# Reordering the start of a fused state-space and two-layer kernel, and loading a broadcast matrix in two transfers

## The chip, the cores and the metric

The kernel runs on one core of a Trainium2 chip. A core has five engines with a queue of instructions each: TensorE (PE in the profile; its weight loads stand apart as PEld), VectorE (DVE), ScalarE (ACT), GpSimd (POOL) and SyncE (SP), which here only issues DMAs. Sixteen DMA engines move data between HBM and SBUF. The metric is the device time of one execution in microseconds; the kernel before takes 588.4 us (median of 3 runs, 588.01 to 589.73).

## The reference

Three parts follow each other; all arithmetic is in float32, and no part may be left out.

```python
# 1. attn: x [4, 8, 768, 32], a [4, 8, 768], B and C [4, 8, 768, 16], in chunks of 32 positions
cum = cumsum(log(clip(a, 1e-6, 1)))                        # within a chunk
L = exp(cum_i - cum_j) * (i >= j)
y = ((C B^T) * L) x  +  (C state) * exp(cum)
state = exp(cum_last) * state + sum_j B_j x_j * exp(cum_last - cum_j)
x = y.transpose(0, 2, 1, 3).reshape(3072, 256)
# 2. first layer: w_in [256, 2048], w_out [2048, 256]
h = x @ w_in;  g = where(h > 0, h, exp(min(h, 0)) - 1);  x = g @ w_out
# 3. second layer: w1, w2 [256, 1024], w3 [1024, 1024], w_out [1024, 256]
out = ((x @ w1) * (x @ w2)) @ w3 @ w_out
```

## The kernel before

The 3072 rows are worked on in six tiles of 512 (`TT`), and a tile is made of four chunks of 128 positions (24 chunks in all, two halves of 64 in each). TensorE gets its float32 operands as two words, a high part that it can take at its full rate and the rest: `split` (lines 102 to 104) rounds on ScalarE and subtracts on VectorE or GpSimd, and `mm3` (lines 239 to 242) makes three matmuls of one product.

A chunk goes through four phases (lines 416 to 442): `p0` scans the decays into L (`at_prep`) and scales B with L's last column (`bd`), `p1` multiplies C B^T with L (`at_cb`), `p2` scales C with the decays (`at_cd`, on GpSimd) and advances the two states (`at_u`), `p3` makes y from L and from the states and splits it into xT (`at_y`). Phase p of chunk k has the number 4k + p in `ORDER` (line 37), the list by which the four chunks of the first tile and the first weights are woven; "pr" is the scan of the first tile's decays, "aw" the matmuls that spread a over chunks 2 and 3, and "h" the first half of the first products.

L of the first four chunks comes from such matmuls. From chunk 4 on `at_l` (lines 306 to 312) loads it: each of a chunk's two halves has one row of 512 values in DRAM (`a_cut`), which all 64 partitions of the half get. It is one DMA, whose source has the loops 2 x 64 (a broadcast) x 512. L has three buffers, the chunks' data (`xbc`, 512 KB) four. `p0` of chunk k issues the loads of L for chunk k + 2 and of the data for chunk k + 3.

Weights arrive as 64-bit words in pieces of 512 KB (class `Piece`, lines 121 to 158), and each goes through three stages: `load` (the DMA), `bits` (a shift on VectorE, a scaling on ScalarE, a merge on VectorE) and `parts` (`split`). `queue` holds the pieces in the order in which the steps need them: w_in 0, 1, 2, w_out 0, w_in 3, w_out 1 and so on. An entry (i, stage) of `ORDER` brings piece i up to that stage (2 is `bits`, 3 is `parts`); reaching 3 also issues the load of piece i + 8, which takes the room of an earlier one. The other stages come from `weights_for` (lines 609 to 616), by due times in a planner's clock.

After the attention of the first tile the steps run: unit a (12 matmuls of 512 columns, then exponential, ramp and maximum on ScalarE and VectorE, and a split to g), unit b (12 matmuls into an accumulator), and later c, d and w. The first tile's eight a and b units run with the chunks of the second tile and the weights' stages placed between.

Each engine's instructions run in the order in which a scheduler wrote them, from a simulation of this program. `pace` (lines 115 to 119) tells it to keep an instruction behind the latest mark; marks are the last entries of `last_mm` after each entry of `ORDER` and after each step. `at_prep`, `at_cb` and `at_y` put their VectorE result there for the first four chunks; `at_u` leaves what was there.

Of the kernel before, what the change touches and what calls it, by code (L numbers as in the profile page):

```python
# [10 lines left out]
ALU = mybir.AluOpType  # L11
AX = mybir.AxisListType

NB, NH, S, D, N = 4, 8, 768, 32, 16
Q = 128
SUB = 2
R = Q // SUB
CPB = S // Q
NCHUNK = NB * CPB
TT = 512  # L20
NTILE = NB * S // TT
CPT = TT // Q
# [11 lines left out]
PACE, LATE, END, FIRST = 1.5, 12.0, 7.0, 8.0  # L34
SPILL, BACK = 3, 8

ORDER = [0, 4, 1, "pr", 2, "aw", (0, 2), 5, 3, 6, (0, 3), 8, 7, 9, (1, 2), 10, 12, 11, 13, (1, 3), 14, "h", 15, (2, 2), (3, 2)]


XCOLS = (("x", DM), ("bn", NH * N), ("bt", 2 * R), ("cz", 2 * 2 * R), ("cp", SUB * 2 * R))  # L40
# [3 lines left out]
def kernel(  # L44
# [20 lines left out]
    nc = tc.nc  # L65
# [9 lines left out]
    V, A, G, T = nc.vector, nc.scalar, nc.gpsimd, nc.tensor  # L75
# [23 lines left out]
    def pair(shape, name, tag=None):  # L99
        return [wts.tile(shape, F32R, name=f"{name}_{p}", tag=f"{tag or name}_{p}") for p in ("hi", "lo")]  # L100

    def split(hi, lo, raw, lo_eng):
        A.copy(hi, raw)  # L103
        return lo_eng.tensor_tensor(out=lo, in0=raw, in1=hi.bitcast(F32), op=ALU.subtract)  # L104

    def tmp(name):
        return act.tile([P, 2, TT], F32, tag="tmp", name=name, bufs=TMP)

    def banks(name):

        return ps_w.tile([P, 2, TT], F32, tag="w", name=name)
# [48 lines left out]
    w_in_s = pair([P, 2, F1], "w_in")  # L160
# [7 lines left out]
    early = [0]  # L168
# [68 lines left out]
    last_mm = []  # L237

    def mm3(out, whi, wlo, xhi, xlo, first, last, **kw):
        last_mm[:] = [T.matmul(out, wlo, xhi, start=first, stop=False, **kw).ins]  # L240
        T.matmul(out, whi, xlo, start=False, stop=False, **kw)  # L241
        T.matmul(out, whi, xhi, start=False, stop=last, **kw)  # L242
# [12 lines left out]
    xT = {}  # L255
    state = {}
    a_cut = tc.dram_tile([NCHUNK * SUB, NH, R], F32, name="a_cut")
# [17 lines left out]
    def at_load(k):  # L275
        c = ck[k]
        all_ = att.tile([P, XC], F32, tag="xbc", name=f"xbc{k}", bufs=4)
        nc.sync.dma_start(all_, xc[k])
        cols_ = {}
        at = 0  # L280
        for nm, n in XCOLS:
            cols_[nm] = all_[:, at:at + n]
            at += n
        c["x"], c["bn"] = cols_["x"], cols_["bn"].rearrange("p (h n) -> p h n", h=NH)
        c["bt"] = cols_["bt"].rearrange("p (g j) -> p g j", g=2)
        c["cz"] = cols_["cz"].rearrange("p (g f) -> p g f", g=2)
        c["cp"] = cols_["cp"].rearrange("p (s f) -> p s f", s=SUB)

    pr = {}

    def at_pr(t):

        pr[t] = att.tile([P, CPT * SUB, R], F32, tag="pr", name=f"pr{t}", bufs=2)
        nc.sync.dma_start(pr[t].rearrange("p k i -> p (k i)"),
                          a_h[t].rearrange("h (o s) -> h o s", o=1).to_broadcast([NH, N, TT]))

    def at_decay(t):

        v = pr[t]
        pace(clip(V, v, v))  # L300
        V.tensor_copy(begun[:, :, 0:1], v[:, :, 0:1])
        V.memset(v[:, :, 0:1], 0.0)
        V.tensor_tensor_scan(out=v.rearrange("p k i -> p (k i)"), data0=v.rearrange("p k i -> p (k i)"),
                             data1=begun.rearrange("p k i -> p (k i)"), initial=0.0, op0=ALU.mult, op1=ALU.add)

    def at_l(k):
        c = ck[k]
        c["L"] = att.tile([P, NH, R], F32, tag="L", name=f"L{k}", bufs=3)
        if k >= CPT:
            nc.sync.dma_start(c["L"].rearrange("p h s -> p (h s)"),  # L310
                              a_cut[SUB * k:SUB * k + SUB].rearrange("s h (o i) -> s o (h i)", o=1)
                              .to_broadcast([SUB, R, NH * R]))

    def at_wide(k):


        wide = ps_a.tile([P, 2, TT], F32, tag="acc", name=f"aw{k}") if k else banks(f"aw{k}")
        for j in range(2):
            for p in range(2):
                mm = T.matmul(wide[:, j], sel[:, k + j].rearrange("r s i -> r (s i)"),  # L320
                              cut[0][:, p].rearrange("r h i -> r (h i)"), start=p == 0, stop=p == 1)
                if j == p == 0:
                    tc.keep_in_program_order(mm)
            ck[k + j]["a"] = wide[:, j]
# [44 lines left out]
    def at_u(k):  # L369


        c = ck[k]
        last = k % CPB == CPB - 1
        u = banks(f"u{k}")
        for p in range(4):
            for s in range(SUB - last):
                rows = slice(R * s, R * s + R)
                T.matmul(u[32 * p:32 * p + 32, s, :2 * D], c["bd"][rows, 2 * p:2 * p + 2].rearrange("p h n -> p (h n)"),
                         c["x"][rows, 64 * p:64 * p + 64], start=True, stop=True)
        for s in range(SUB - last):  # L380
            new = att.tile([P, 2 * D], F32, tag="st", name=f"st{k}_{s}", bufs=4)
            if k % CPB or s:
                V.scalar_tensor_tensor(out=new, in0=state[k, s], scalar=c["pr"][:, s, R - 1:R], in1=u[:, s, :2 * D],
                                       op0=ALU.mult, op1=ALU.add)
            else:
                V.tensor_copy(new, u[:, s, :2 * D])
            state[(k, 1) if s == 0 else (k + 1, 0)] = new

    def at_y(k):
        c = ck[k]  # L390
        both = banks(f"y{k}")[:, :, :2 * R].rearrange("p s (g i) -> p s g i", g=2)


        for g in range(2):
            for s in range(SUB):
                rows = slice(R * s, R * s + R)
                for q in range(4):
                    h = 2 * q + g
                    mm = T.matmul(both[32 * q:32 * q + 32, s, g], c["x"][rows, D * h:D * h + D], c["L"][rows, h],
                                  start=g == 0, stop=(k, s) not in state, skip_group_check=True)  # L400
        for g in range(2):
            for s in range(SUB):
                for q in range(4) if (k, s) in state else ():
                    rows = slice(32 * q, 32 * q + 32)
                    mm = T.matmul(both[rows, s, g], state[k, s][rows, D * g:D * g + D], c["cd"][rows, s, g],  # L405
                                  start=False, stop=True, skip_group_check=True)
        last_mm[:] = [mm.ins]
        t, s0 = k // CPT, (k % CPT) * Q
        if k % CPT == 0:
            xT[t] = [act.tile([P, 2, TT], F32R, tag=f"xx{p}", name=f"xT{p}{t}", bufs=3) for p in ("h", "l")]  # L410
        made = split(*(v[:, :, s0:s0 + Q].rearrange("p g (s i) -> p s g i", s=SUB) for v in xT[t]), both, V)
        if k < CPT:
            last_mm[:] = [made.ins]
# [29 lines left out]

    gt, pt, x2, accs = {}, {}, {}, {}

    early_h = []

    def products(h, t, n, cs):
        for j in range(2):
            fs = slice((2 * n + j) * P, (2 * n + j + 1) * P)  # L450
            for k in range(2):
                mm3(h[:, j, cs], w_in_s[0][:, k, fs], w_in_s[1][:, k, fs], xT[t][0][:, k, cs], xT[t][1][:, k, cs],
                    k == 0, k == 1)

    def first_half():

        early_h.append(banks("h0_0"))
        products(early_h[0], 0, 0, slice(0, TT // 2))

    def unit_a(t, n):  # L460

        early = early_h and (t, n) == (0, 0)
        h = early_h[0] if early else banks(f"h{t}_{n}")
        products(h, t, n, slice(TT // 2 if early else 0, TT))
        e = tmp(f"e{t}_{n}")
        A.activation(e, h, AF.Exp)  # L466

        A.activation(e, e, AF.Relu, scale=-1.0, bias=1.0)  # L468
        V.scalar_tensor_tensor(out=e, in0=e, scalar=-1.0, in1=h, op0=ALU.mult, op1=ALU.max)  # L469
        g = act.tile([P, 2, 2, TT], F32R, tag="g", name=f"g{t}_{n}")  # L470
        split(g[:, 0], g[:, 1], e, V)
        gt[t, n] = g
# [64 lines left out]
    made = 0  # L537
# [107 lines left out]
    constants()  # L645
    at_load(0)
    at_pr(0)
    queue[0].advance(1)
    for k in range(1, CPT):
        at_load(k)  # L650
    for p in queue[1:3]:
        p.advance(1)
# [3 lines left out]
    for k in range(CPT):  # L656
        at_l(k)
# [3 lines left out]

    for j in ORDER:
        if j == "pr":
            at_decay(0)
        elif j == "aw":
            at_wide(2)
        elif j == "h":
            first_half()
        elif isinstance(j, tuple):
            i, stage = j  # L670
            queue[i].advance(stage)
            if stage == 3:
                load_next(i)
        else:
            attn[j]()
            marks.extend(last_mm)
    at_pr(1)
    for k in range(CPT, CPT + LOADS):
        if k < CPT + LOADS - 1:
            at_l(k)  # L680
        at_load(k)
# [67 lines left out]
```

## Time and profile before

| | |
|---|---|
| median of 3 runs | 588.4 us |
| the profiled execution | 588.74 us |
| its span, first to last instruction | 587.0 us |
| TensorE busy | 560.5 us, 95% of the span |
| VectorE busy | 336.2 us, 57% |
| ScalarE busy | 277.7 us, 47% |
| GpSimd busy | 83.8 us, 14% |
| loads of L | 20 of 256 KB |
| mean granted TensorE clock | 0.991 of 2.4 GHz |

A row of the timeline gives start and duration in us, the engine, the line of the kernel, the operation, the tile written and those read (their numbers left out), the shapes and how many instructions were merged into the row; in brackets stands the idle time of the engine ahead of it and what ended that. TensorE's matmuls are pipelined, so their distance from start to start is what counts. `L` alone is the decay matrix; `L333` is line 333.

### The profile page before, as it was taken

How to read it: one execution, taken by the hardware profiler on the slowest of the kernel's cores; microseconds unless marked ns; L12 is line 12 of the kernel's file. 1: busy time of each engine (PE TensorE's matmuls, PEld its weight loads, DVE VectorE, ACT ScalarE, POOL GpSimd, SP SyncE). 2: the span in 40 equal slices, each digit the busy share in tenths (PEclk: the TensorE clock that was granted, in tenths of full speed). 3: DMA queues.
4: the chain of work that ended last, by engine and by line, in shares of the span. 5: the costliest groups of instructions: out<-in, count | busy, mean ns of one | idle time of the engine just before them, and what ended most of it. 6: DMA issues, size and time to landing. Idle time of an engine off the chain costs nothing.

```text
span 587.0 us, 10429 instructions
## 1 busy us (share of the span) xinstructions
PE 560.5 (95%) x4436; PEld 439.8 (75%) x4436; DVE 336.2 (57%) x468; ACT 277.7 (47%) x390; POOL 83.8 (14%) x91
## 2 busy tenths in 40 slices
PE   5986799999999999999999999999999999999996
PEld 3665577767877888887788787887777778888784
DVE  6697879677675865668433335343676353335332
ACT  2294567565564655775323223232454552355222
POOL 2201114322222312253000000000021000000000
PEclk9999699999999999999999999999999999999999
DMA  8885353724453331621013031100110000010000
GB/s 297 298 242 155 124 173 111 260 101 126 137 195 96 113 127 73 214 86 58 1 50 113 1 126 37 54 37 1 58 53 1 1 1 0 1 37 2 0 1 36
DMA packets 26567, 52.78 MB, mean 90 GB/s; under 512 B 1592, under 2 KB 9784, under 8 KB 26520
## 3 DMA queue, kind: packets, MB, share of 16 engines
q1 hardware_dynamic: 26520, 52.11, 27.1%
q8 instruction: 35, 0.57, 0.4%
q14 instruction: 12, 0.10, 0.1%
HBM read 45.71 MB, written 6.39 MB: 89 GB/s over the span
## 4 chain that ended last, share of the span: by engine, by line
PE 77%; DMA 10%; DVE 6%; ACT 2%; issue 2%; POOL 1%; SPq 0%; POOLq 0%; DVEq 0%; ACTq 0%
PE ab L240 8%; PE ab L241 7%; PE ab L242 7%; DMA L<-a_cut 6%; PE acc_b L240 6%; PE acc_b L241 6%; PE h L240 6%; PE acc_b L242 6%; PE h L242 5%; PE h L241 5%; PE acc_d L240 4%; PE acc_d L241 4%; PE acc_d L242 4%; PE y L405 2%; DMA raw_wc<-in_w3t 2%
## 5 line engine op out<-in xcount | busy, mean ns | idle before, releaser
L469 DVE SCALAR_TENSOR_TENSOR e<-e,h 128x1024 f32<-128x1024 f32 x48 | 58.4, 1216 | 39.8 <-ACT e L468 39.8
L241 PE MATMUL acc_b<-g,w_out_hi 128*128 128x512 f32 x192 | 77.3, 403 | 3.8 <-DVE g L104 3.8
L240 PE MATMUL acc_b<-g,w_out_lo 128*128 128x512 f32 x192 | 77.9, 406 | 3.1 <-DVE w_out_lo L104 2.1
L240 PE MATMUL h<-xTh,w_in_lo 128*128 128x512 f32 (+1 forms) x196 | 78.1, 399 | 1.9 <-DVE e L469 1.0
L104 DVE TENSOR_TENSOR g<-e,g 128x1024 fp32r<-128x1024 f32 x48 | 61.6, 1283 | 29.0 <-ACT g L103 28.7
L242 PE MATMUL h<-xTh,w_in_hi 128*128 128x512 f32 (+1 forms) x196 | 76.2, 389 | 0.0
L241 PE MATMUL h<-xTl,w_in_hi 128*128 128x512 f32 (+1 forms) x196 | 76.2, 389 | 0.0
L242 PE MATMUL acc_b<-g,w_out_hi 128*128 128x512 f32 x192 | 76.1, 396 | 0.0
L240 PE MATMUL ab<-x2h,w 128*128 128x512 f32 x192 | 74.6, 394 | 0.7 <-ACT x2h L103 0.7
L241 PE MATMUL ab<-x2l,w 128*128 128x512 f32 x192 | 75.0, 391 | 0.0
L103 ACT CAST g<-e 128x1024 fp32r<-128x1024 f32 x48 | 50.4, 1050 | 52.0 <-DVE e L469 38.1
L242 PE MATMUL ab<-x2h,w 128*128 128x512 f32 x192 | 74.8, 389 | 0.0
L466 ACT ACTIVATE e<-h 128x1024 f32<-128x1024 f32 x48 | 49.2, 1026 | 44.2 <-PE h L242 43.0
L514 DVE TENSOR_TENSOR pa<-pa,ab 128x512 f32<-128x512 f32 x48 | 32.6, 684 | 61.2 <-ACT pa L513 61.2
L513 ACT COPY pa<-ab 128x512 f32<-128x512 f32 x48 | 27.9, 589 | 74.4 <-PE ab L242 73.5
L104 DVE TENSOR_TENSOR p<-pa,p 128x512 fp32r<-128x512 f32 x48 | 32.9, 692 | 34.2 <-ACT p L103 33.8
L468 ACT ACTIVATE e<-e 128x1024 f32<-128x1024 f32 x48 | 51.0, 1063 | 0.9
L103 ACT CAST p<-pa 128x512 fp32r<-128x512 f32 x48 | 29.8, 622 | 44.9 <-PE acc_d L242 23.3
L366 POOL TENSOR_TENSOR cd<-xbc,pr 128x256 f32<-128x256 f32 x24 | 24.7, 1028 | 173.9 <-issue 85.8
L240 PEld LDWEIGHTS acc_b<-g,w_out_lo 128*128 128x128 f32 x192 | 36.6, 190 | 13.1 <-DVE w_out_lo L104 2.5
L241 PEld LDWEIGHTS acc_b<-g,w_out_hi 128*128 128x128 f32 x192 | 36.6, 191 | 12.8 <-DVE g L104 5.2
L240 PEld LDWEIGHTS h<-xTh,w_in_lo 128*128 128x128 f32 x196 | 37.2, 190 | 11.5 <-DVE e L469 1.5
(93 smaller groups left out, 898.5 us busy)
## 6 DMA issues: line engine op xcount, KB each, us to landing
xbc<-in_xc SPq DMA_DIRECT2D x24, 512.0 KB, 9.8
raw_wc<-in_w3t SPq DMA_DIRECT2D x16, 512.0 KB, 7.0
L<-a_cut SPq DMA_DIRECT2D x20, 256.0 KB
raw_wi<-in_w_in SPq DMA_DIRECT2D x8, 512.0 KB, 11.9
raw_wo<-in_w_out SPq DMA_DIRECT2D x8, 512.0 KB
out_t<-o SPq DMA_DIRECT2D x12, 256.0 KB, 2.0
raw_wq<-in_wo SPq DMA_DIRECT2D x4, 512.0 KB, 11.5
raw_wb<-in_w SPq DMA_DIRECT2D x4, 512.0 KB
```

The lines of the kernel that those rows point to most:

```text
L103: A.copy(hi, raw)
L104: return lo_eng.tensor_tensor(out=lo, in0=raw, in1=hi.bitcast(F32), op=ALU.subtract)
L240: last_mm[:] = [T.matmul(out, wlo, xhi, start=first, stop=False, **kw).ins]
L241: T.matmul(out, whi, xlo, start=False, stop=False, **kw)
L242: T.matmul(out, whi, xhi, start=False, stop=last, **kw)
L366: G.tensor_tensor(out=c["cd"], in0=c["cp"].rearrange("p s (w i) -> p s w i", w=2), in1=c["pr"].rearrange("p s (o i) -> p s o i", o=1).to_b ...
L405: mm = T.matmul(both[rows, s, g], state[k, s][rows, D * g:D * g + D], c["cd"][rows, s, g], start=False, stop=True, skip_group_check=True)
L466: A.activation(e, h, AF.Exp)
L468: A.activation(e, e, AF.Relu, scale=-1.0, bias=1.0)
L469: V.scalar_tensor_tensor(out=e, in0=e, scalar=-1.0, in1=h, op0=ALU.mult, op1=ALU.max)
L513: A.copy(e, h[:, 0])
L514: V.tensor_tensor(out=e, in0=e, in1=h[:, 1], op=ALU.mult)
```

## The change

There are five edits:

- the early half of the first products goes ("h" in `ORDER`, `first_half`, and the split of `unit_a` in two halves of columns);
- `at_u` sets the mark for the first four chunks, so that paced stages of weights which follow in `ORDER` are kept behind the chunk's last state;
- piece 2 (w_in 2) goes through `bits` and `parts` and piece 3 (w_out 0) through both as well around the last y of the tile; before, only their `bits` stood there, behind that y;
- the data of chunk 1 is loaded ahead of the first piece of weights;
- L of a chunk is loaded by two DMAs of 64 partitions, one for each half.

```diff
-ORDER = [0, 4, 1, "pr", 2, "aw", (0, 2), 5, 3, 6, (0, 3), 8, 7, 9, (1, 2), 10, 12, 11, 13, (1, 3), 14, "h", 15, (2, 2), (3, 2)]
+ORDER = [0, 4, 1, "pr", 2, "aw", (0, 2), 5, 3, 6, (0, 3), 8, 7, 9, (1, 2), 10, 12, 11, 13, (1, 3), 14, (2, 2), (2, 3), 15, (3, 2), (3, 3)]
...
         if k >= CPT:
-            nc.sync.dma_start(c["L"].rearrange("p h s -> p (h s)"),
-                              a_cut[SUB * k:SUB * k + SUB].rearrange("s h (o i) -> s o (h i)", o=1)
-                              .to_broadcast([SUB, R, NH * R]))
+
+            for s in range(SUB):
+                nc.sync.dma_start(c["L"][R * s:R * s + R].rearrange("p h s -> p (h s)"),
+                                  a_cut[SUB * k + s:SUB * k + s + 1].rearrange("s h i -> s (h i)").to_broadcast([R, NH * R]))
...
             if k % CPB or s:
-                V.scalar_tensor_tensor(out=new, in0=state[k, s], scalar=c["pr"][:, s, R - 1:R], in1=u[:, s, :2 * D],
-                                       op0=ALU.mult, op1=ALU.add)
+                made = V.scalar_tensor_tensor(out=new, in0=state[k, s], scalar=c["pr"][:, s, R - 1:R], in1=u[:, s, :2 * D],
+                                              op0=ALU.mult, op1=ALU.add)
             else:
-                V.tensor_copy(new, u[:, s, :2 * D])
+                made = V.tensor_copy(new, u[:, s, :2 * D])
             state[(k, 1) if s == 0 else (k + 1, 0)] = new
+        if k < CPT:
+            last_mm[:] = [made.ins]
...
-    def first_half():
-
-        early_h.append(banks("h0_0"))
-        products(early_h[0], 0, 0, slice(0, TT // 2))
...
-        early = early_h and (t, n) == (0, 0)
-        h = early_h[0] if early else banks(f"h{t}_{n}")
-        products(h, t, n, slice(TT // 2 if early else 0, TT))
+        h = banks(f"h{t}_{n}")
+        products(h, t, n)
...
     at_pr(0)
+    at_load(1)
     queue[0].advance(1)
-    for k in range(1, CPT):
+    for k in range(2, CPT):
         at_load(k)
```

## Rows read from the trace of the kernel before

**Rows 1.** The page: busy tenths of TensorE and VectorE in 40 slices of 14.7 us.

```profile
PE   5986799999999999999999999999999999999996
DVE  6697879677675865668433335343676353335332
```

**Rows 2.** Stages: length, busy us of PE, PEld, DVE, ACT, POOL; clock, DMA share, GB/s.

```profile
30.00:50.00 20.00, 16.52 (x134) 11.91 (x132) 19.84 (x29) 17.59 (x24) 2.05 (x2) 1.00 0.75 217
50.00:60.00 10.00, 6.09 (x58) 4.66 (x50) 6.12 (x11) 2.43 (x4) 2.06 (x3) 0.92 0.62 189
60.00:70.00 10.00, 7.89 (x78) 5.65 (x79) 8.36 (x12) 5.45 (x8) 1.03 (x2) 0.57 0.21 78
150.00:200.00 50.00, 50.00 (x489) 39.74 (x488) 35.63 (x50) 29.85 (x39) 11.28 (x12) 1.00 0.44 139
```

**Rows 3.** The chain of waits, start and length in us, from 19 to 57 us.

```profile
19.86 21.72 DMA L<-a_cut
...
41.64 15.33 DMA L<-a_cut
```

**Rows 4.** The timeline of SyncE, 18 to 31 us.

```profile
18.13 6.73 SPq L310 DMA_DIRECT2D L<-a_cut  x2
24.96 5.05 SPq L278 DMA_DIRECT2D xbc<-in_xc  x1
30.11 0.48 SPq L136 DMA_DIRECT2D raw_wo<-in_w_out  x1
```

**Rows 5.** Stages as in rows 2: chunks and weights loading, then only L.

```profile
18.00:20.00 2.00, 1.47 (x59) 0.86 (x56) 1.99 (x4) 0.56 (x1) 0.45 (x1) 1.00 1.04 382
54.60:56.70 2.10, 1.47 (x29) 0.88 (x27) 0.00 (x0) 0.00 (x0) 0.00 (x0) 1.00 0.13 52
```

**Rows 6.** The timeline of VectorE, 9.5 to 13 us.

```profile
9.50 0.42 DVE L261 TENSOR_SCALAR pr<-pr 128x512 f32<-128x512 f32 x1
9.83 0.42 DVE L146 TENSOR_SCALAR raw_wi<-raw_wi 128x512 uint32<-128x512 uint32 x1
...
10.47 0.68 DVE L148 SCALAR_TENSOR_TENSOR raw_wi<-raw_wi 128x512 uint32<-128x512 uint32 x1
...
11.21 1.22 DVE L303 TENSOR_TENSOR_SCAN pr<-pr,begun 128x512 f32<-128x512 f32 x1
12.35 0.67 DVE L104 TENSOR_TENSOR w_in_lo<-raw_wi,w_in_hi 128x512 fp32r<-128x512 f32 x1
```

**Rows 7.** The timeline of VectorE, 23 to 82 us.

```profile
23.53 0.59 DVE L383 SCALAR_TENSOR_TENSOR st<-st,pr,u 128x64 f32<-128x64 f32 x2
28.09 0.42 DVE L104 TENSOR_TENSOR xTl<-y,xTh 128x256 fp32r<-128x256 f32 x1 [3.97 <-ACT xTh L103]
...
57.00 1.22 DVE L333 TENSOR_TENSOR_SCAN L<-L,eye 128x512 f32<-128x512 f32 x1 [3.88 <-DMA L<-a_cut]
...
62.49 0.68 DVE L104 TENSOR_TENSOR w_out_lo<-raw_wo,w_out_hi 128x512 fp32r<-128x512 f32 x1
...
66.87 1.23 DVE L333 TENSOR_TENSOR_SCAN L<-L,eye 128x512 f32<-128x512 f32 x1 [1.64 <-DMA L<-a_cut]
...
81.88 0.42 DVE L104 TENSOR_TENSOR xTl<-y,xTh 128x256 fp32r<-128x256 f32 x1 [2.08 <-ACT xTh L103]
```

**Rows 8.** The timeline of TensorE, 25 to 65 us.

```profile
25.93 0.68 PE L399 MATMUL y<-L,xbc 64*32 64x64 f32 x32
...
59.98 1.13 PE L351 MATMUL cb<-xbc 32*64 32x128 f32 x16 [3.91 <-issue]
63.22 0.79 PE L240 MATMUL acc_b<-g,w_out_lo 128*128 128x512 f32 x1 [2.11 <-DVE w_out_lo L104]
...
64.24 0.63 PE L242 MATMUL acc_b<-g,w_out_hi 128*128 128x512 f32 x1
64.67 0.63 PE L240 MATMUL acc_b<-g,w_out_lo 128*128 128x512 f32 x1
```

**Rows 9.** The timeline of ScalarE at 30 us.

```profile
30.21 1.04 ACT L466 ACTIVATE e<-h 128x1024 f32<-128x1024 f32 x1
```

More of the change, by code (lines that the diff above doesn't have):

```diff
@@ L444, with products @@
     gt, pt, x2, accs = {}, {}, {}, {}
-    early_h = []
-    def products(h, t, n, cs):
+    def products(h, t, n):
         for j in range(2):
@@ L451, in products @@
             for k in range(2):
-                mm3(h[:, j, cs], w_in_s[0][:, k, fs], w_in_s[1][:, k, fs], xT[t][0][:, k, cs], xT[t][1][:, k, cs],
-                    k == 0, k == 1)
-    def first_half():
-        early_h.append(banks("h0_0"))
-        products(early_h[0], 0, 0, slice(0, TT // 2))
+                mm3(h[:, j], w_in_s[0][:, k, fs], w_in_s[1][:, k, fs], xT[t][0][:, k], xT[t][1][:, k], k == 0, k == 1)
     def unit_a(t, n):
-        early = early_h and (t, n) == (0, 0)
-        h = early_h[0] if early else banks(f"h{t}_{n}")
-        products(h, t, n, slice(TT // 2 if early else 0, TT))
+        h = banks(f"h{t}_{n}")
+        products(h, t, n)
         e = tmp(f"e{t}_{n}")
@@ L666 @@
             at_wide(2)
-        elif j == "h":
-            first_half()
         elif isinstance(j, tuple):
```

## The prediction

> **What bounds the kernel now.** I read the page first. Of TensorE's forty digits only the first five slices (73 us) hold anything but nines: 5, 9, 8, 6, 7 [rows 1]. So only the head can give something. A table by stages confirms it: from 150 us on TensorE fills its stretch (50.00 of 50.00), while in 50 to 60 it works 6.09 of 10 us and in 60 to 70 the granted clock is 0.57 [rows 2]. What TensorE does after 70 us moves as one block; the question is how much sooner the head delivers it.
>
> In the head I followed the chain of waits. It holds two pieces of pure transfer: L from a_cut, 21.72 us from 19.86, and the next L, 15.33 us from 41.64 [rows 3]. Each moves 256 KB. SyncE's timeline shows the same from the other side: the two L issues at 18.13 hold it for 6.73 us, and the chunk data behind them hold it another 5.05 us [rows 4]. Then I asked for a stretch in which only L is under way: from 54.6 to 56.7 us the DMA share is 0.13, that is 2 of 16 engines, at 52 GB/s, against 1.04 and 382 GB/s while whole chunks and weights are loaded [rows 5]. So a load of L as written runs on two engines, and whatever is queued behind it is complete only when those two get to it.
>
> VectorE's timeline says what that costs. VectorE stands still for 3.97 us before 28.09, for 3.88 us before the scan of L at 57.00 and for 1.64 us before the next one at 66.87, the last two for L's transfer [rows 7]. Around these it is near full (digits 9, 7, 8 from 29 to 73 us [rows 1]). So VectorE bounds the head, twice interrupted by L. TensorE follows it: it waits 3.91 us until 59.98 and 2.11 us until 63.22, and then runs at 1.2 GHz, its 512-column matmuls 0.43 us apart at 64.24 [rows 8].
>
> **The change part by part.** I add up on VectorE's line, because that sets the end of the head.
>
> *The first weight piece's stages behind the first chunk's states.* Now its shift at 9.83 and its merge at 10.47 stand ahead of the decay scan at 11.21 [rows 6], on which cd, the first y and so all later chunks wait. They take 0.42 + 0.68 us, less some 0.09 of overlap each (9.50 + 0.42 against 9.83): 0.9 us. Behind the states they fall into VectorE's short idle stretches. I take 0.9 us gained; the bounds are -0.5 (the work displaces something in the next chunk instead) and 1.5 (the third step, 0.67 us at 12.35, leaves the path too).
>
> *Chunk 1's data ahead of the first weights.* 512 KB at 382 GB/s [rows 5] is 1.4 us, by which the weights land later. Their shift now runs at 9.83; it is then wanted only behind the scan, over 12 us, so some 2 us cover the delay. Without that cover it would cost 1.4 us.
>
> *No early half of the first products.* Removed are 12 matmuls of 256 columns which stand on TensorE ahead of the tile's last y, until 25.93 [rows 8]. That y needs the states, done at 24.12 [rows 7], and its chunk's L, done half a microsecond before; its first half could start at about 23.6 and, with the 0.9 us from above, at 22.7. It takes 1.7 us (two groups from 25.93), its two splits 0.8, so xTl stands at about 25.2 where it now ends at 28.5 [rows 7]. The products are then 12 of 512 columns from about 24.9: at 0.43 us each [rows 8] they end at 30.1, which is where the second half ends now (the exponential starts at 30.21 [rows 9]); at the full level, at half that price, they would end at 27.5. I take no gain and no loss for TensorE here; bounds 0 and 2.
>
> *Pieces 2 and 3 between the states and that y.* VectorE's idle 3.97 us is the wait for this y. Two pieces at about 1.5 us each (shift, merge and difference, 0.3 + 0.6 + 0.6 without the overlap, by rows 6) fill it, or follow right behind the earlier xTl. New idle time appears: behind xTl VectorE has some 4.9 us of weight work (four pieces, 1.3 us of it already done), until 30.1, and its next part of the activation needs the exponential (1.04 us [rows 9]) and the ramp, another such: 30.2 + 2.1 = 32.3. Of those 2.2 us the next piece's bits take about 1.0; with 0.6 us ahead of xTl I count 1.8 us lost again. So 3.97 - 1.8 = 2.2 us; bounds -1.0 (the weight steps in front of xTl on ScalarE and VectorE hold the products) and 3.5.
>
> *L in two transfers.* As written the source's outer loop has two rows, and two engines work; the chunk data, whose outer loop is 128 partitions on both sides, reach 1.04 of 16 [rows 5]. In the change source and target both have 64 in the outer loop. The cost of the new form is bounded by two engines again (262 KB at 52 GB/s: 5.0 us, and as much waiting behind them as now) and by the chunk data's rate (262 KB at 382 GB/s: 0.7 us). I take it near the second, as 64 is like 128 and not like 2. Then the L issued at 41.64 is there long before 53.1, when VectorE comes to it, and the waits of 3.88 and 1.64 us [rows 7] go: 5.5 us; bounds 0 and 5.5.
>
> The Trainium skill, "DMA: Bandwidth & Descriptors", section "Why a DMA increments its semaphore by 16 and not by 1", says that a transfer uses the largest number of engines up to 16 that divides the outermost loop of both sides. For the loads of before that is two, and the share of 0.13 [rows 5] agrees; for the new form it is 16, which no row shows yet. By it the sum stands; if the row's two engines held for each half as well, 5.5 us would come off.
>
> Twenty more issues of about 0.5 us (0.48 us at 30.11 is an unhindered one [rows 4]) stand on SyncE ahead of chunk data and weights. SyncE has that time once the holds of 5 us are gone; uncovered it would be 0.5 us a chunk, 2 us over the head.
>
> What is late next: TensorE waits until 63.22 for VectorE's w_out_lo (62.49 [rows 7]), and its half-clock stretch (12 x 0.43 us where the full level needs half: 2.6 us) hides in that wait or goes with it, so I don't add it. After 70 us VectorE has slack (2.08 us before 81.88 [rows 7]): what the head gains is kept.
>
> Sum: 0.9 + 2.2 + 5.5 = 8.6 us. The profiled execution took 588.7 us (span 587.0 and 1.7 around it), 0.3 above the median of the runs shown: 580.1 on its scale, 579.8 on that of the medians.
>
> **The rivals** (on the scale of the medians).
>
> *TensorE sets the end; a larger gain.* If VectorE finds work in all its gaps and the clock stays up, TensorE's own losses count: 3.91 + 2.11 + 2.6, the 3.5 us that it misses in 30 to 50 us [rows 2], and 0.9 + 0.6 ahead: 13.6 us, 574.8. For it: TensorE is dense from 70 us on. Against: VectorE's digits in the head.
>
> *The wait moves; a small gain.* VectorE works strictly in its written order, and that order is made anew. Between the scan at 57.00 and the w_out_lo that TensorE wanted, 5.5 us of other work stood [rows 7]. If such a run stands in front of TensorE again, a hole of 3 us and the 2.6 us of half clock come back: of 8.6 some 3.0 are left, 585.4.
>
> *The two transfers don't spread.* Then L's landing sets VectorE's time as now, and what is gained ahead of it is eaten by that wait: some 1 us is left, 587.4. Against it: the outer loop of 64.
>
> *Slower: the clock.* The early half was TensorE's first dense work, and from 30 to 50 us the level was 1.00 in spite of 3.5 us of holes [rows 2]. Without that half the dense work starts later and, as VectorE paces it, with holes; the level may stay at 1.2 GHz through the first a and b units. Each 512-column matmul then costs 0.21 us more. Beyond 41 of them (8.6 / 0.21), three and a half units of 12, the change loses; if five and a half of the eight units before 56 us run so, 65 matmuls, it costs 13.7 us, 5.1 net: 593.5. For it: the level did fall at the one long hole (0.57 in 60 to 70). Against: it held in 30 to 50.
>
> The Trainium skill, "TensorE: Matmul & The Clock Gate", section "What's actually happening", calls the throttled level the default, which activity releases. The 0.57 behind the hole [rows 2] agrees. By it, taking early dense work away speaks against the change, and 593.5 is what that would give.
>
> **How the numbers follow.** Forecast 0.50 (577 to 583), larger gain 0.15, small gain 0.21, no spread 0.06, slower 0.08. Within 0.3% (1.8 us, about what a measurement of this kernel can tell from no change) lie the no-spread case and a little of the small one: 0.08. Faster 0.84, slower 0.08. The range goes from a little beyond the larger gain (573.5, with TensorE's 2 us of the first products in part) to where the small gain shades into none (587.0).
>
> **What would show it.** Right: no L transfer in the chain of waits; where L moves, a DMA share near 1 in a short burst and no hold of 5 us on SyncE; VectorE idle for under 1 us before the tile's fourth xTl and not at all before a scan of L; granted clock 1.00 in 50 to 70. Wrong: a scan of L still released by its transfer; a hole of over 3 us on TensorE between 30 and 70 us with a fallen clock; the exponential of the first products later than 30.21.

## The result, and the profile after

The changed kernel takes 583.5 us (median of 5 runs, 582.95 to 585.75); the kernel before, run beside it, takes 588.6 (5 runs). The ratio is 0.9918, 95% interval 0.9895 to 0.9941: 5.1 us gained, where 8.6 were forecast. The profiled execution of the changed kernel is the longest of its five (585.75 us, span 583.9), so what follows compares moments in the head. The spans of the two profiled executions are only 3.1 us apart (587.0 before); where the rest went stands at the end of this section.

The page of the changed kernel: the digits of TensorE, and the chain of waits by engine.

```profile
PE   5797998999999999989999999999999999999996
...
PE 78%; DVE 10%; DMA 3%; issue 3%; ACT 3%; POOL 1%; SPq 0%; DVEq 0%; POOLq 0%
```

Against rows 1, the third to fifth digits of TensorE (29 to 73 us) have risen, from 8, 6, 7 to 9, 7, 9; the second (15 to 29 us), in which the early half of the first products stood, has fallen from 9 to 7. An 8 is new in the eighteenth slice (248 to 263 us). The chain has 3% of DMA, against 10% on the page of before, and no L among the transfers in it.

SyncE's timeline after, and the row of L among the DMA issues (count, KB each, median us from issue to landing):

```profile
19.27 5.46 SPq L312 DMA_DIRECT2D L<-a_cut  x4
26.36 0.35 SPq L278 DMA_DIRECT2D xbc<-in_xc  x1
...
48.03 0.37 SPq L136 DMA_DIRECT2D raw_wo<-in_w_out  x1
48.51 1.09 SPq L312 DMA_DIRECT2D L<-a_cut  x2
```

```profile
L<-a_cut SPq DMA_DIRECT2D x40, 128.0 KB, 3.6
```

Half an L lands 3.6 us (median) after its issue, where the two loads in [rows 3] took 15 and 22; the chunk data behind the first ones hold SyncE for 0.35 us instead of 5.05 [rows 4]. (The 5.46 us at 19.27 are four issues with waits between them; none of the four takes more than 0.51.) The stages (columns as in rows 2): in the first of them an L and the w_out piece issued at 48.03 move, in the last an L alone (only packets of 2 KB, the length of a row of L):

```profile
49.60:50.60 1.00, 1.00 (x6) 0.82 (x5) 1.00 (x3) 0.00 (x0) 0.51 (x1) 1.00 0.98 377
...
50.00:60.00 10.00, 7.29 (x70) 5.25 (x69) 10.00 (x17) 6.26 (x9) 2.90 (x3) 0.86 0.50 167
60.00:70.00 10.00, 10.00 (x116) 7.30 (x115) 7.71 (x13) 4.68 (x8) 1.15 (x2) 0.80 0.34 120
...
65.80:66.80 1.00, 1.00 (x6) 0.84 (x5) 1.00 (x3) 0.00 (x0) 0.00 (x0) 1.00 0.62 203
```

The DMA share is 0.98 with a w_out piece beside L, and 0.62 with L alone, where L alone had 0.13 [rows 5]. VectorE is now full from 50 to 60 us (10.00 instead of 6.12 [rows 2]); from 60 to 70 TensorE is (10.00 instead of 7.89), at a granted clock of 0.80. VectorE's timeline after:

```profile
10.28 1.22 DVE L303 TENSOR_TENSOR_SCAN pr<-pr,begun 128x512 f32<-128x512 f32 x1
...
11.73 0.86 DVE L146 TENSOR_SCALAR raw_wi<-raw_wi 128x512 uint32<-128x512 uint32 x1
...
14.73 0.68 DVE L358 TENSOR_TENSOR L<-cb,L 128x512 f32<-128x512 f32 x1
...
25.43 0.69 DVE L104 TENSOR_TENSOR w_in_lo<-raw_wi,w_in_hi 128x512 fp32r<-128x512 f32 x1 [0.71 <-ACT w_in_hi L103]
26.50 0.42 DVE L104 TENSOR_TENSOR xTl<-y,xTh 128x256 fp32r<-128x256 f32 x1 [0.38 <-ACT xTh L103]
...
32.95 0.69 DVE L148 SCALAR_TENSOR_TENSOR raw_wi<-raw_wi 128x512 uint32<-128x512 uint32 x1 [0.84 <-ACT raw_wi L147]
...
51.85 1.21 DVE L334 TENSOR_TENSOR_SCAN L<-L,eye 128x512 f32<-128x512 f32 x1
...
57.32 0.68 DVE L104 TENSOR_TENSOR w_out_lo<-raw_wo,w_out_hi 128x512 fp32r<-128x512 f32 x1
...
59.45 1.21 DVE L334 TENSOR_TENSOR_SCAN L<-L,eye 128x512 f32<-128x512 f32 x1
...
69.08 0.69 DVE L104 TENSOR_TENSOR w_in_lo<-raw_wi,w_in_hi 128x512 fp32r<-128x512 f32 x1 [1.63 <-ACT w_in_hi L103]
```

Against rows 7: the two scans of L have no idle time ahead of them and stand 5.15 and 7.42 us earlier; the xTl of the tile's fourth chunk stands 1.6 us earlier. TensorE's timeline after, and ScalarE's exponentials:

```profile
15.47 0.68 PE L402 MATMUL y<-L,xbc 64*32 64x64 f32 x32 [1.95 <-DVE L L358]
...
25.00 1.06 PE L408 MATMUL y<-cd,st 32*32 32x64 f32 x28 [0.83 <-issue]
26.52 1.22 PE L240 MATMUL h<-xTh,w_in_lo 128*128 128x512 f32 x2 [0.46 <-ACT xTh L103]
...
28.82 0.63 PE L241 MATMUL h<-xTl,w_in_hi 128*128 128x512 f32 x1
29.25 0.63 PE L242 MATMUL h<-xTh,w_in_hi 128*128 128x512 f32 x1
...
58.06 0.80 PE L240 MATMUL acc_b<-g,w_out_lo 128*128 128x512 f32 x1 [2.71 <-DVE w_out_lo L104]
58.65 0.63 PE L241 MATMUL acc_b<-g,w_out_hi 128*128 128x512 f32 x1
59.08 0.63 PE L242 MATMUL acc_b<-g,w_out_hi 128*128 128x512 f32 x1
...
64.43 0.50 PE L240 MATMUL h<-xTh,w_in_lo 128*128 128x512 f32 x1
```

```profile
31.34 1.03 ACT L460 ACTIVATE e<-h 128x1024 f32<-128x1024 f32 x1 [0.30 <-PE h L242]
...
67.48 1.02 ACT L460 ACTIVATE e<-h 128x1024 f32<-128x1024 f32 x1 [3.17 <-PE h L242]
```

The unit that waits for w_out_lo starts at 58.06 instead of 63.22 [rows 8], 5.16 us earlier, about as much as the median gained. But ahead of it stands a hole of 2.71 us, and behind it its matmuls are 0.43 us apart, as they were before.

The rest of the kernel does not simply keep these 5.16 us. The lead grows to 6.20 us at the first product of the second layer (`ab`), by a route that was not followed, and is then partly lost. TensorE's timeline there, before:

```profile
264.31 0.39 PE L240 MATMUL ab<-x2h,w 128*128 128x512 f32 x1
...
266.84 0.50 PE L241 MATMUL acc_b<-g,w_out_hi 128*128 128x512 f32 x1 [0.78 <-DVE g L104]
```

After:

```profile
258.11 0.39 PE L240 MATMUL ab<-x2h,w 128*128 128x512 f32 x1
...
261.93 0.80 PE L241 MATMUL acc_b<-g,w_out_hi 128*128 128x512 f32 x1 [2.08 <-DVE g L104]
262.52 0.63 PE L242 MATMUL acc_b<-g,w_out_hi 128*128 128x512 f32 x1
262.95 0.63 PE L240 MATMUL acc_b<-g,w_out_lo 128*128 128x512 f32 x1
```

VectorE's timeline after says what the `g` waited for:

```profile
260.32 0.43 DVE L146 TENSOR_SCALAR raw_wa<-raw_wa 128x512 uint32<-128x512 uint32 x1 [3.31 <-DMA raw_wa<-in_w]
```

A weight piece of the second layer, issued at 253.58 us, now ends VectorE's wait; in the kernel before VectorE waited there for GpSimd. The hole has grown from 0.78 to 2.08 us and matmuls behind it are 0.43 us apart: of the 6.20 us of lead, 3.3 are left. The changed kernel was profiled a second time (an experiment below, 583.42 us). There the same hole is 1.66 us long and the level does not fall (granted clock 1.00 from 255 to 265 us, against 0.85 here):

```profile
261.15 0.50 PE L241 MATMUL acc_b<-g,w_out_hi 128*128 128x512 f32 x1 [1.66 <-DVE g L104]
```

Of a lead of 6.6 us 5.7 are left in it, and its span is 581.6. So the gain in the median is what the head gives, less 0.9 to 2.9 us in these two profiles at 260 us.

### The profile page after: what moved, and what is told of

Same layout as the page of the kernel before. It is cut to its first block, busy times and chain, and to the rows that moved or that the text cites. A ratio compares the mean times of both kernels' runs of the same rounds, so it can differ in the third digit from the quotient of the medians.

```text
span 583.9 us, 10471 instructions
## 1 busy us (share of the span) xinstructions
PE 559.5 (96%) x4424; PEld 439.8 (75%) x4424; DVE 335.0 (57%) x468; ACT 278.0 (48%) x390; POOL 83.2 (14%) x91
## 4 chain that ended last, share of the span: by engine, by line
PE 78%; DVE 10%; DMA 3%; issue 3%; ACT 3%; POOL 1%; SPq 0%; DVEq 0%; POOLq 0%
PE ab L240 8%; PE ab L241 7%; PE ab L242 7%; PE acc_b L240 6%; PE acc_b L241 6%; PE h L240 6%; PE acc_b L242 6%; PE h L242 5%; PE h L241 5%; PE acc_d L240 4%; PE acc_d L241 4%; PE acc_d L242 4%; DMA raw_wa<-in_w 2%; PE y L408 2%; PE cb L352 2%
## 5 line engine op out<-in xcount | busy, mean ns | idle before, releaser
L240 PE MATMUL h<-xTh,w_in_lo 128*128 128x512 f32 x192 | 77.5, 404 | 1.6 <-DVE e L463 1.1
L241 PE MATMUL h<-xTl,w_in_hi 128*128 128x512 f32 x192 | 75.4, 392 | 0.0
L242 PE MATMUL h<-xTh,w_in_hi 128*128 128x512 f32 x192 | 75.3, 392 | 0.0
```

## The experiments

Theory: the spread of L over all DMA engines is the whole gain. Rival: the other edits (order, marks, the missing early half) bring a share of their own, or cost one. The first four runs share 17 runs of the kernel before (median 589.0 us).

**L in two transfers alone**, in the kernel before:

```diff
-                nc.sync.dma_start(c["L"]..., a_cut[SUB * k:SUB * k + SUB] ... .to_broadcast([SUB, R, NH * R]))
+            for s in range(SUB):
+                nc.sync.dma_start(c["L"][R * s:R * s + R]..., a_cut[SUB * k + s:SUB * k + s + 1] ... .to_broadcast([R, NH * R]))
```

> The kernel before with one part of the change alone: L in two transfers of 64 partitions. Theory (the spread of L over the DMA engines is what the change gains): the waits of 3.88 and 1.64 us for L vanish and 4 to 5.5 us are gained, 583.1 to 584.6 against 588.6. Rival (the new order of the start gains, L was only in its way): at most 1 us, 587.6 or more.

582.85 us (4 runs), ratio 0.9893 (0.9878 to 0.9908): 6.2 us, at least as much as the whole change. VectorE's timeline of this kernel:

```profile
27.33 0.42 DVE L104 TENSOR_TENSOR xTl<-y,xTh 128x256 fp32r<-128x256 f32 x1 [3.13 <-ACT xTh L103]
...
52.30 1.21 DVE L334 TENSOR_TENSOR_SCAN L<-L,eye 128x512 f32<-128x512 f32 x1
```

The wait ahead of xTl is still there (3.13 us, 3.97 in rows 7), as the order of before is, and yet the scan comes 4.7 us earlier than at 57.00 [rows 7].

**The whole change with L in one transfer** (the same diff, reversed, in the changed kernel):

> The changed kernel with L in one transfer again, everything else changed. Theory: VectorE's waits for L come back and eat what the new order gains ahead of them; 587.5 to 589.0, no change from before. Rival (the order gains): 584 to 586.

589.58 us (12 runs), ratio 1.0011 (0.9997 to 1.0025): nothing. Its VectorE timeline has the waits for L back, longer than in rows 7:

```profile
58.11 1.22 DVE L333 TENSOR_TENSOR_SCAN L<-L,eye 128x512 f32<-128x512 f32 x1 [5.50 <-DMA L<-a_cut]
...
67.98 1.22 DVE L333 TENSOR_TENSOR_SCAN L<-L,eye 128x512 f32<-128x512 f32 x1 [2.16 <-DMA L<-a_cut]
```

So with the old L the other edits bring nothing: VectorE reaches the scan at 52.6 (58.11 less 5.50) and waits longer. TensorE's hole of 3.91 us [rows 8] is back too, with 5.67 us. With the new L they bring nothing that can be told either, as 0.9893 and 0.9918 overlap.

**Is it the number of transfers, or their outer loop?** Two transfers for each L, but the outer loop of each source has two rows again, so each half of L's partitions is filled from two sub-blocks.

```diff
-                                  a_cut[SUB * k + s:SUB * k + s + 1].rearrange("s h i -> s (h i)").to_broadcast([R, NH * R]))
+                                  a_cut[r:r + 2].rearrange("s h (o i) -> s o (h i)", o=1).to_broadcast([2, R // 2, NH * R]))
```

> The changed kernel, L still in two transfers of 64 partitions, but each reads two neighbouring rows of a_cut for 32 partitions each, so that the source's outer loop is 2 again (half of each L then holds the neighbour's values: the output is not the reference's). Theory (the outer loop of 2 keeps a transfer on two engines, their number does not matter): a DMA share of 0.13 while only L moves, waits for L back, 587.5 to 589.5. Rival (splitting in two is what spreads it): 583.5 within 1 us.

594.09 us (6 runs), ratio 1.009 (1.0073 to 1.0106), with the wait for L of before, and in a stretch in which nothing else moves (stages, columns as in rows 2) the share of before:

```profile
58.02 1.23 DVE L336 TENSOR_TENSOR_SCAN L<-L,eye 128x512 f32<-128x512 f32 x1 [5.11 <-DMA L<-a_cut]
```

```profile
56.00:58.00 2.00, 0.00 (x0) 0.00 (x0) 0.00 (x0) 0.00 (x0) 0.00 (x0) 1.00 0.13 51
```

The page of each kernel counts packets under 512 B: of before (and the same with L in one transfer again), of this one, and of the changed kernel:

```profile
DMA packets 26567, 52.78 MB, mean 90 GB/s; under 512 B 1592, under 2 KB 9784, under 8 KB 26520
DMA packets 26607, 52.78 MB, mean 89 GB/s; under 512 B 1632, under 2 KB 9824, under 8 KB 26560
DMA packets 27167, 52.78 MB, mean 90 GB/s; under 512 B 2192, under 2 KB 10384, under 8 KB 27120
```

For each of the 20 L this is 2 packets more with two transfers of two rows, and 30 more with two transfers of 64. One small packet for each engine that a transfer uses would give just that: 2 for an L of before, 2 x 2 here, 2 x 16 in the changed kernel. It is the outer loop. That this kernel is 4.5 us slower than the one-transfer form was not expected; against that form it has twenty more transfers, each on two engines, but how they cost the time was not followed.

**The early half put back** into the changed kernel, run twice (in a first and in a third group):

```diff
-ORDER = [... (1, 3), 14, (2, 2), (2, 3), 15, (3, 2), (3, 3)]
+ORDER = [... (1, 3), 14, "h", (2, 2), (2, 3), 15, (3, 2), (3, 3)]
...
+    def first_half():
+        early_h.append(banks("h0_0"))
+        products(early_h[0], 0, 0, slice(0, TT // 2))
```

> The changed kernel with the early half of the first products put back in front of the tile's last y. Theory: in the changed kernel the first products end at 31.1 us, 1 us later than before, so the removal gained nothing; 583.5 within 1 us. Rival 1 (the removal gained by the earlier y): 585.5 or more. Rival 2 (the removal cost, because TensorE's clock now rises 2 us later): 582 or less.

581.58 us (6 runs), ratio 0.9884 (0.9862 to 0.9906).

> The changed kernel with the early half of the first products kept, beside the changed kernel on one chip. Theory (the half is done in time in which TensorE would stand idle, and its removal puts 12 full matmuls at 1.2 GHz behind the y): 1.5 to 2 us faster than the run before this one. Rival (the 1.9 us found earlier were the difference between two chips): no difference beyond 0.7 us.

582.70 us (6 runs), ratio 0.9878 (0.9852 to 0.9905), beside the changed kernel itself:

> The changed kernel itself, on one chip with the next two, so that they can be compared directly. Every theory: 0.991 of before, some 583.5 to 585.

583.30 us (6 runs), ratio 0.9890 (0.9868 to 0.9912). The removal may cost some 0.6 us (583.30 less 582.70), which this scatter can't tell from nothing. One thing the removal did take away: in both profiles with the early half the granted clock is 1.00 from 50 to 70 us, as TensorE's wait there falls into two (1.6 and 0.8 us) with matmuls between; in both profiles of the changed kernel it is one wait of 2.7 us, and the clock 0.86 and 0.80, 0.87 and 0.79. Of the executions with the early half (these two runs and the last below), 9 of 18 show a mean granted clock of 1.000, of the changed kernel's 11 none. The two profiles of the one program with the early half show where scatter comes from. TensorE's timeline of the first, then of the second, both with 256 columns a matmul:

```profile
28.27 0.28 PE L242 MATMUL h<-xTh,w_in_hi 128*128 128x256 f32 x1
28.39 0.28 PE L240 MATMUL h<-xTh,w_in_lo 128*128 128x256 f32 x1
```

```profile
28.61 0.41 PE L241 MATMUL h<-xTl,w_in_hi 128*128 128x256 f32 x1
28.82 0.42 PE L242 MATMUL h<-xTh,w_in_hi 128*128 128x256 f32 x1
```

0.12 us apart in one, 0.21 in the other: matmuls of the same unit at the paces of 2.4 and of 1.2 GHz. The exponential behind them starts at 29.66 and at 31.20 us, and the spans are 580.0 and 581.3.

**Does the half clock behind the hole swallow the second wait?** The changed kernel with 24 matmuls of 256 columns that nobody reads, put in the hole ahead of the unit at 58.06:

```diff
         last_mm[:] = [mm.ins]
+        [T.matmul(cb[:, i % 2, 4 * R:], w_in_s[0][:, 0, :P], xT[0][0][:, 0, :4 * R], start=True, stop=True, ...) for i in range(24 if k == CPT + 1 else 0)]
```

> The changed kernel with 24 matmuls of 256 columns that nobody reads, behind the C B^T of chunk 5, where TensorE has a hole of 2.71 us at 55.35 (they write columns of that tile which are otherwise unused). Theory (the clock that falls in this hole makes TensorE the bound from 58 to 64 us and swallows what VectorE gains on the second L): granted clock 1.00 through 50 to 70 us, the 12 matmuls from 58 us 0.23 us apart, 2 us gained, 581.5. Rival (VectorE sets the time from 58 us too): the clock stays up and the time stays at 583.5 within 0.7.

582.67 us (4 runs), ratio 0.988 (0.986 to 0.9901; the kernel before at 590.28 beside it), not the 2 us of gain that the theory expected. TensorE's timeline of this kernel:

```profile
56.29 3.13 PE L356 MATMUL cb<-xTh,w_in_hi 128*128 128x256 f32 x24
59.26 0.40 PE L240 MATMUL acc_b<-g,w_out_lo 128*128 128x512 f32 x1
59.49 0.40 PE L241 MATMUL acc_b<-g,w_out_hi 128*128 128x512 f32 x1
...
63.82 0.46 PE L402 MATMUL y<-L,xbc 64*32 64x64 f32 x32 [0.95 <-DVE L L358]
...
64.79 0.50 PE L240 MATMUL h<-xTh,w_in_lo 128*128 128x512 f32 x1
```

The unit's matmuls are 0.23 us apart now, and from its start to the next h it takes 5.5 us instead of 6.4 (64.43 less 58.06). TensorE does not win the whole difference: it waits 0.95 us for VectorE instead. The unit itself starts 1.2 us later than in the changed kernel's profile (59.26 against 58.06); 1.05 of them VectorE brought along (its w_out_lo starts at 58.37 against 57.32). The median is not told apart from the changed kernel's. So the half clock is real as a bound there, and worth about 0.8 us in these two profiles.

**Marks, engines and the first product.** Four more: the first is one edit of the changed kernel, the others are one edit each of the kernel with the early half put back.

The changed kernel without the mark in `at_u`:

```diff
-        if k < CPT:
-            last_mm[:] = [made.ins]
```

> The changed kernel without the mark set by the states of the first four chunks. Theory (as measured in the trace, the mark moved the decay scan up by 0.9 us but the first piece's steps then stood before the product of chunk 1; about 0.5 us net): 584.0. Rival 1 (the full 0.9 us and more): 584.5 or above. Rival 2 (the mark cost time): 583.0 or below.

583.76 us (6 runs), ratio 0.9897 (0.9875 to 0.9919): the mark does nothing to the median that can be measured.

With the early half, and the difference of the w_in pieces (and of one w_out piece) on GpSimd instead of VectorE from the seventh piece of the queue on:

```diff
     for p in queue[:first_n]:
-        p.lo = V
+    for j, p in enumerate(queue[:first_n]):
+        p.lo = V if j < 6 or j % 2 else G
```

> The changed kernel with the early half kept (581.6), and the difference (last step) of w_in pieces 4 to 7 and of one more from the seventh entry of the queue on given to GpSimd instead of VectorE. Theory (VectorE bounds the head from 36 to 73 us, TensorE's holes there add up to 5.3 us): five steps of 0.6 us off VectorE, 2 us gained, 579.5. Rival (the holes come from the order of the steps, or GpSimd's 1.3 to 1.8 us a step makes weights late): 581.6 or more.

583.38 us (5 runs), ratio 0.9884 (0.9862 to 0.9907): no gain, where the theory expected 2 us. The same for the w_out pieces, from the eighth on (`j % 2 == 0`):

> As the one before, but the w_out pieces from the eighth entry of the queue on go to GpSimd. Theory (VectorE's load is what counts): the same 579.5. Rival (w_out is what TensorE waits for at the holes, so the slower engine on it costs): 582 or more, with waits of TensorE for w_out_lo from GpSimd.

584.10 us (6 runs), ratio 0.9905 (0.9883 to 0.9928). TensorE now waits for GpSimd at the place where it waited for VectorE:

```profile
58.23 0.50 PE L240 MATMUL acc_b<-g,w_out_lo 128*128 128x512 f32 x1 [2.52 <-POOL w_out_lo L104]
```

The unit starts at 58.23, between the 58.46 and 59.93 of the two profiles with the early half alone: taking VectorE's work off brought nothing that can be told from scatter. Last, with the early half, the first piece's steps behind chunk 1's product on VectorE:

```diff
-ORDER = [0, 4, 1, "pr", 2, "aw", (0, 2), 5, 3, ...]
+ORDER = [0, 4, 1, "pr", 2, "aw", 5, (0, 2), 3, ...]
```

> As the run before this one (early half kept), with the first weight piece's steps one place further back, behind chunk 1's product of C B^T and L; on VectorE only that product changes its place. Theory (the 2.05 us hole of TensorE before the y of chunk 1 is this piece, standing in front of the product; the decay scan's gain of 0.9 us was lost there): 1 us faster than the run before this one, the hole under 1 us. Rival (the time is found again further on, since the chain of the four chunks waits elsewhere): no difference beyond 0.5 us.

582.18 us (6 runs, 580.00 to 585.45), ratio 0.9877 (0.9844 to 0.991). In TensorE's timeline of this kernel chunk 1's y starts without the hole of 1.95 us, 2.2 us earlier than at 15.47:

```profile
13.24 0.76 PE L402 MATMUL y<-L,xbc 64*32 64x64 f32 x32
```

The hole is explained; whether closing it gains 0.5 us or nothing is below the scatter of these runs. Most of that scatter goes with the clock: the three executions with a mean granted clock of 1.000 took 580.0 to 580.9 us, the three at 0.991 to 0.993 took 583.5 to 585.5.

## Why the prediction was right, and where it was too high

**L in two transfers.** Right in mechanism, and exact in its larger part. The Trainium skill's rule on the outermost loops ("DMA: Bandwidth & Descriptors", section "Why a DMA increments its semaphore by 16 and not by 1") held both ways: with 64 in the outer loop the share is 0.62 with L alone and the small packets fit 16 engines, with two it is 0.13. The wait of 3.88 us [rows 7] is gone whole: of the 5.15 us by which the first scan came earlier it is 3.88, and 1.27 came from ahead of it.

**The second wait for L (1.64 us)** is the step that failed in that term: it was counted as gained on the path. It went from VectorE, whose scan stands 7.42 us earlier, but not from the path. I wrote that TensorE's half-clock stretch "hides in that wait or goes with it". It did neither: the hole of 2.71 us was left (2.11 before [rows 8]), the level fell again behind it, and from 58 to 64 us TensorE at 1.2 GHz became the bound. VectorE then idles 1.63 us ahead of 69.08, the old loss under another name: it waits for ScalarE, which itself waited 3.17 us, until 67.48, for TensorE's h. The next h comes 5.05 us earlier (64.43 against 69.48), no more than the unit ahead of it. That is the mechanism of the small-gain rival, at one place: a hole of 2.7 us and the half clock came back. The kernel with the unread matmuls agrees with it, as far as its 0.8 us go.

**"What the head gains is kept"** is the other step that failed. The reason given was VectorE's slack after 70 us, and the opening let TensorE's work behind that move "as one block". It did not: the lead of 5.05 us at 64 us was 6.20 at 258 us, and a weight piece's load, which did not end a wait there before, took 2.9 of them back at 260 us (0.9 of 6.6 in the second profile). What the head outruns is a wait that the sum has no term for.

**Pieces 2 and 3 around the last y (2.2 us), and the first piece's stages (0.9 us).** Mis-sized: together they and the earlier chunk data gave the 1.27 us at the scan, instead of 3.1; and of these, L's spread alone gave 0.8 (the scan at 52.30, 4.70 less 3.88). What is left for the two terms is some 0.5 us, and the medians show none of it. The parts:

- The decay scan came 0.93 us earlier (10.28 against 11.21 [rows 6]), as worked out. But the piece's three steps (from 11.73 on) now stand ahead of chunk 1's product at 14.73, and TensorE waits 1.95 us for that. The fourth chunk's states come 0.54 us earlier (22.99 against 23.53 [rows 7]), not 0.9. My lower bound had named this ("displaces something in the next chunk instead"); I took the other value.
- I let the last y start at 22.7 and xTl end at 25.2. It starts at 23.13, stops for 0.83 us in mid-run (at 24.17) with no wait that the profile shows, and xTl ends at 26.9. So VectorE's 3.97 us became 0.71 and 0.38 ahead of xTl, and 0.84 and some shorter ones behind it.
- The exponential starts at 31.34, later than 30.21 [rows 9]. That was my sign of an error, and it came: the first products run 0.43 us apart until about 29.7, and there are twelve full ones now. In the kernel before, the early half had done half of them by 26 us. My "no gain and no loss" for TensorE was thus some 1.1 us too good there.

**Slower by the clock.** Its place was real but small: the lower pace held on for the first seven matmuls of 512 columns, and for about as many behind the hole at 260 us in the first profile, far from the 41 beyond which the change would have lost. The twelve behind the hole at 58 us stood at that pace before, too.

**Direction and chances.** The measured 583.5 us lie just outside the 577 to 583 that had a chance of 0.50, on the side of the small gain (0.21). No L in the chain, a share near 1 in short bursts, no hold of 5 us, no wait at a scan: these signs came. "Granted clock 1.00 in 50 to 70" did not, with 0.86 and 0.80; it marked the first failing step. That the 5.1 us come close to the 5.5 of L's term is in part luck: one of its two waits counted for nothing, an amount that no term named was added before 258 us, and the hole at 260 us took some back.

## What to carry to other kernels

When a load looks slow, ask for a stretch in which it moves alone and count its share in engines: a share of 2 in 16 came from an outer loop of 2, and rewriting the source's loops was worth more than all reordering. A wait that is taken from one engine counts only as far as the next engine isn't slowed in the same stretch: look at whether the hole that drops the clock is gone as well, before the wait is added to the sum. A stretch that is pulled ahead is pulled ahead of its loads as well: look for the first load that was in time by less than the gain. Where steps are moved behind one consumer, look for the next product that they now stand in front of.

## What was not expected of the hardware

The moment at which TensorE's pace doubles in the head is not a property of the program: one program ran the same matmuls at either level at the same place, and with it its head shifted by 1.5 us and its span by 1.3. The hole at 260 us does the same a second time: the two profiles of the changed kernel are within 0.4 us of each other at 258 us and 2.35 us apart behind it, the level having fallen in one (hole of 2.08 us) and not in the other (1.66). Edits of 0.5 to 1 us in the head can't be told apart by medians of six runs with this under them (580.0 to 585.5 us in one kernel). At 28 us the clock column reads 1.00 in both; the distance of the matmuls is what shows it.

TensorE's stop of 0.83 us inside the last y at 24.17 follows no wait in the trace. It is no accident of one execution: the second profile of the changed kernel has it with 0.83 us too, those with the unread matmuls, with L in one transfer and with two rows have it with 0.91, 0.63 and 1.46, while none with the early half has it, nor the one without the mark. What it is stays open.
